# Loading k and v for two heads at a time from another DMA queue, with a reordered last tile, in a low-rank attention decode kernel

## The chip, the cores and the metric

The kernel runs on one core of one Trainium2 chip. The metric is the device time of one execution, in microseconds (us), as the median of several executions. The span of a profile runs from the first to the last instruction of one execution; the measured time exceeds it by about 1.7 to 2.2 us.

PE is TensorE, the matrix engine; DVE, ACT, POOL and SP are VectorE, ScalarE, GpSimd and SyncE. An eviction copies a matmul's result (vp_a, say) into a tile that a later matmul reads (vp_a_sb). A load has landed when all 16 DMA engines have reported their share of it.

## The reference

```python
B, H, Sq, Skv, Dh, R = 1, 16, 1, 8192, 256, 16          # all bf16
kp = einsum("rn,bhnd->bhrd", e_proj, k)                 # 16 x 256 per head
vp = einsum("rn,bhnd->bhrd", f_proj, v)
scores = einsum("bhqd,bhrd->bhqr", q, kp) * Dh ** -0.5
o = einsum("bhqr,bhrd->bhqd", softmax(scores), vp)      # 1 x 256 per head
```

Every byte of k and v is read once: 16 heads, two tensors, 4 MB each, 134.2 MB in all. The arithmetic on it is small. A tuned kernel can therefore only be as fast as its loads, plus what comes before the first byte and after the last one.

## The kernel before

A head's 8,192 rows lie on 128 partitions, 64 consecutive rows on each, so one partition's share is a run of 32 KB. All k and v tiles come from GpSimd's DMA queue into five buffers of 4 MB. The last head's k is loaded first and its v last, in pieces.

```python
KV_BUFS = 5;  RING = "gpsimd"                            # kv_dma = nc.gpsimd
def load_full(dst, src_head):
    kv_dma.dma_start(out=dst[:], in_=src_head.rearrange("(p j) d -> p j d", j=J))   # J = 64

def proj_pairs(acc_a, acc_b, w_t, kt):
    for j in range(JH):                                  # JH = 32: rows j and j + 32 side by side
        j2 = j + JH
        nc.tensor.matmul(acc_a[0:R, :], lhsT=w_t[:, j, :], rhs=kt[:, j, :],
                         start=(j == 0), stop=(j == JH - 1), tile_position=(0, 0))
        nc.tensor.matmul(acc_b[32:32 + R, :], lhsT=w_t[:, j2, :], rhs=kt[:, j2, :],
                         start=(j2 == JH), stop=(j2 == J - 1), tile_position=(0, 32))
# ... k_phase: evict both halves, transpose, add, scores, softmax, transpose p (one head) ...
def v_phase(h, vt, pT_a, pT_b):
    proj_pairs(vp_a, vp_b, f_t, vt)
    # ... evict vp_a and vp_b, two products with p, copy, add into o_sb[:, h, :] ...

# ... the other 15 heads: k_phase, v_phase, loads issued ahead ...
bounds = [0, JH, JH + JH // 2, J - 4, J]                 # the last tile: 0, 32, 48, 60, 64
for a, b in zip(bounds[:-1], bounds[1:]):
    kv_dma.dma_start(out=vt_last[:, a:b, :], in_=v_last[:, a:b, :])
v_phase(h_first, vt_last, pT_first[0], pT_first[1])
nc.sync.dma_start(out=..., in_=o_sb)                     # 8 KB
```

The two matmuls of a step sit in different column tiles of the array and run at the same time (in the trace a pair starts within 0.01 us, as at 66.44 us).

## Time and profile before

| | before |
|---|---|
| median time | 330.81 us (4 runs) |
| span | 329.1 us |
| the k/v queue's packets, share of the time of 16 DMA engines | 96.1% |
| first load packet / last load packet | 2.62 / 321.98 us |
| PE busy, DVE busy | 61%, 19% |

Lines of the profile page of the kernel before: span, busy time by engine, the span in 40 slices (DMA is the busy share of the 16 DMA engines in tenths), queues (packets, MB, share) and the chain that ended last by engine.

```profile
span 329.1 us, 4843 instructions
PE 200.8 (61%) x2210; PEld 139.2 (42%) x2210; DVE 63.1 (19%) x228; ACT 7.0 (2%) x33; POOL 21.9 (7%) x44
...
DMA  7999999999999999999999999999999999999970
GB/s 259 383 442 432 406 438 440 436 402 435 440 446 408 426 440 438 416 426 438 436 422 420 438 436 430 424 430 440 415 431 432 442 408 434 432 442 418 413 312 4
...
q0 software_dynamic: 5168, 134.75, 96.1%
q8 instruction: 17, 0.28, 0.3%
...
DMA 83%; PE 14%; issue 1%; DVE 1%; POOL 0%; POOLq 0%
```

DMA is at nine tenths or more in all slices but the first and the last two. So the middle of this kernel is bound by the rate of the DMA engines, and only the two ends are open to a change. The line of q8: 17 packets of 16 KB in which the engines' own instructions are fetched by the same DMA engines.

The chain that ended last, at the end of the kernel before (start us, duration us, what):

```profile
267.82 43.35 DMA vt<-in_v_dram
...
318.80 2.06 PE vp_a L100 x18
...
321.19 0.99 PE vp_b L108 x10
...
323.72 1.86 PE vp_b L108 x16
...
326.37 0.41 DVE o_sb L226
```

The last load packet lands at 321.98 us, but the chain goes back to a load that landed at 311.2, head 14's v. From there on PE has work until 325.6 us, with gaps of about half a microsecond around the evictions: it works off 6.3 us of head 14 (5.3 us of it at half clock), then the last tile. Those 64 matmuls stand in runs of one column tile (x18, x10, x16), where each takes 0.11 us alone instead of 0.11 us for a pair. Then come the evictions and the output:

```profile
322.99 0.41 DVE L208 CAST vp_a_sb<-vp_a 16x256 bf16<-16x256 f32 x1 [3.73 <-PE vp_a L100]
323.76 0.41 DVE L225 COPY o_a_sb<-o_a_ps 1x256 f32<-1x256 f32 x1 [0.36 <-PE o_a_ps L213]
325.60 0.42 DVE L210 CAST vp_b_sb<-vp_b 16x256 bf16<-16x256 f32 x1 [1.43 <-PE vp_b L108]
326.37 0.41 DVE L226 TENSOR_TENSOR o_sb<-o_a_sb,o_b_ps 1x256 bf16<-1x256 f32 x1 [0.35 <-PE o_b_ps L217]
326.81 0.30 SPq L254 DMA_DIRECT2D out_dram<-o_sb  x1
```

(DVE's and SyncE's timeline; in brackets the idle time before, and what ended it.)

### The profile page before, as it was taken

Reading aid. Unit: us, or ns where it says so; the run is one execution under the profiler, and the core shown is the slowest. Engines: PE = TensorE matmul, PEld = TensorE weight load, DVE = VectorE, ACT = ScalarE, POOL = GpSimd, SP = SyncE. Lnnn points to the kernel's source line nnn. Section 1 sums busy time; section 2 is a strip of 40 time slices with the busy share of each in tenths; the row PEclk is TensorE's granted clock in tenths of the full one; section 3 lists DMA queues with packets and bytes.
Section 4 is the critical chain, followed back from the end, with each engine's and each line's share of the span. In section 5 each row is a group of like instructions: output and inputs, shape, how many; then the busy total and the mean of one; then the engine's idle time right before and its main releaser. Section 6 shows DMA issues by size and latency. Waiting matters only on the chain.

```text
span 329.1 us, 4843 instructions
## 1 busy us (share of the span) xinstructions
PE 200.8 (61%) x2210; PEld 139.2 (42%) x2210; DVE 63.1 (19%) x228; ACT 7.0 (2%) x33; POOL 21.9 (7%) x44
## 2 busy tenths in 40 slices
PE   0067545577666576656677564577666666665695
PEld 0044434455444345534454343345434444443463
DVE  0121222210122221122212022221122222012222
ACT  1000000000000000000000000000000000000000
POOL 7000000000000000000000000000000002000000
PEclk9997789875677977767767678977567787776779
DMA  7999999999999999999999999999999999999970
GB/s 259 383 442 432 406 438 440 436 402 435 440 446 408 426 440 438 416 426 438 436 422 420 438 436 430 424 430 440 415 431 432 442 408 434 432 442 418 413 312 4
DMA packets 5190, 135.06 MB, mean 410 GB/s; under 512 B 609, under 2 KB 625, under 8 KB 945
## 3 DMA queue, kind: packets, MB, share of 16 engines
q0 software_dynamic: 5168, 134.75, 96.1%
q8 instruction: 17, 0.28, 0.3%
q14 instruction: 3, 0.02, 0.0%
q1 hardware_dynamic: 2, 0.01, 0.0%
HBM read 134.75 MB, written 0.01 MB: 410 GB/s over the span
## 4 chain that ended last, share of the span: by engine, by line
DMA 83%; PE 14%; issue 1%; DVE 1%; POOL 0%; POOLq 0%
DMA kt<-in_k_dram 40%; DMA vt<-in_v_dram 39%; PE kp_a L100 6%; PE vp_a L100 6%; DMA e_x<-in_e_proj_dram 4%; PE vp_b L108 1%; PE kp_b L108 0%; DVE e_t L61 0%; DVE vp_a_sb L208 0%; POOL kt_first L50 0%; PE o_a_ps L213 0%; PE o_b_ps L217 0%; DVE vp_b_sb L210 0%; DVE o_sb L226 0%; POOLq L272 0%
## 5 line engine op out<-in xcount | busy, mean ns | idle before, releaser
L100 PE MATMUL kp_a<-kt,e_t 128*16 128x256 bf16 x480 | 84.5, 359 | 47.4 <-DMA kt<-in_k_dram 47.4
L100 PE MATMUL vp_a<-vt,f_t 128*16 128x256 bf16 x480 | 84.1, 358 | 14.3 <-DMA vt<-in_v_dram 14.2
L108 PE MATMUL kp_b<-kt,e_t 128*16 128x256 bf16 x480 | 84.6, 360 | 0.0
L108 PE MATMUL vp_b<-vt,f_t 128*16 128x256 bf16 x480 | 84.2, 359 | 0.0
L100 PEld LDWEIGHTS <-e_t 128*16 128x16 bf16 x512 | 59.0, 116 | 50.7 <-DVE e_t L61 16.5
L108 PEld LDWEIGHTS <-e_t 128*16 128x16 bf16 x512 | 58.6, 117 | 42.6 <-issue 42.5
L100 PEld LDWEIGHTS <-f_t 128*16 128x16 bf16 x512 | 58.2, 114 | 21.0
L108 PEld LDWEIGHTS <-f_t 128*16 128x16 bf16 x512 | 57.7, 115 | 15.3 <-issue 14.7
L123 DVE CAST kp_a_sb<-kp_a 16x256 bf16<-16x256 f32 x16 | 6.6, 412 | 117.4 <-PE kp_b L108 117.4
L208 DVE CAST vp_a_sb<-vp_a 16x256 bf16<-16x256 f32 x16 | 6.6, 412 | 97.2 <-PE vp_b L108 93.4
L95 POOL DMA_DIRECT2D kt<-in_k_dram x15 | 8.0, 531 | 125.3 <-PE vp_b L108 110.7
L95 POOL DMA_DIRECT2D vt<-in_v_dram x15 | 7.9, 529 | 122.1 <-PE kp_b L108 112.2
L179 PE MATMUL pT_a_ps<-ident_b,p_b 1*16 1x1 bf16 x16 | 2.7, 166 | 21.4 <-DVE p_b L176 21.4
L100 PE MATMUL kp_a<-kt_first,e_t 128*16 128x256 bf16 x32 | 5.1, 337 | 16.5 <-DVE e_t L61 16.5
L179 PEld LDWEIGHTS <-p_b 1*16 1x16 bf16 x16 | 1.3, 82 | 23.2 <-DVE p_b L176 23.2
L165 ACT ACTIVATE p_f<-s_ps,nbias 1x16 f32<-1x16 f32 x16 | 4.2, 264 | 302.1 <-DVE nbias L162 302.1
L213 PE MATMUL o_a_ps<-vp_a_sb,pT_a 16*1 16x256 bf16 x16 | 4.2, 265 | 8.0 <-DVE vp_a_sb L208 8.0
L130 PE MATMUL psT_a<-ident_b,kp_a_sb 16*128 16x16 bf16 x32 | 3.2, 171 | 7.0 <-DVE kp_a_sb L123 7.0
L210 DVE CAST vp_b_sb<-vp_b 16x256 bf16<-16x256 f32 x16 | 6.7, 417 | 1.9 <-PE vp_b L108 1.4
L226 DVE TENSOR_TENSOR o_sb<-o_a_sb,o_b_ps 1x256 bf16<-1x256 f32 x16 | 6.5, 409 | 1.9 <-PE o_b_ps L217 0.4
L125 DVE CAST kp_b_sb<-kp_b 16x256 bf16<-16x256 f32 x16 | 6.7, 417 | 0.5
L225 DVE COPY o_a_sb<-o_a_ps 1x256 f32<-1x256 f32 x16 | 6.6, 412 | 0.8 <-PE o_a_ps L213 0.4
(40 smaller groups left out, 70.6 us busy)
## 6 DMA issues: line engine op xcount, KB each, us to landing
kt<-in_k_dram POOLq DMA_DIRECT2D x15, 4096.0 KB, 43.0
vt<-in_v_dram POOLq DMA_DIRECT2D x15, 4096.0 KB, 43.1
kt_first<-in_k_dram POOLq DMA_DIRECT2D x1, 4096.0 KB, 12.9
vt_last<-in_v_dram POOLq DMA_DIRECT2D x1, 2048.0 KB, 38.3
vt_last<-in_v_dram POOLq DMA_DIRECT2D x1, 1024.0 KB, 40.2
vt_last<-in_v_dram POOLq DMA_DIRECT2D x1, 768.0 KB, 42.9
e_x<-in_e_proj_dram POOLq DMA_DIRECT2D x1, 256.0 KB, 13.5
f_x<-in_f_proj_dram POOLq DMA_DIRECT2D x1, 256.0 KB, 13.4
```

Source lines behind the costliest of these rows:

```text
L95: kv_dma.dma_start(out=dst[:], in_=src_head.rearrange("(p j) d -> p j d", j=J))
L100: nc.tensor.matmul(acc_a[0:R, :], lhsT=w_t[:, j, :], rhs=kt[:, j, :], start=(j == 0), stop=(j == JH - 1), tile_position=(0, 0),)
L108: nc.tensor.matmul(acc_b[32 : 32 + R, :], lhsT=w_t[:, j2, :], rhs=kt[:, j2, :], start=(j2 == JH), stop=(j2 == J - 1), tile_position=(0, 32),)
L123: nc.vector.tensor_copy(out=kp_a_sb[:], in_=kp_a[0:R, :])
L125: nc.vector.tensor_copy(out=kp_b_sb[32 : 32 + R, :], in_=kp_b[32 : 32 + R, :])
L165: nc.scalar.activation(out=p_f[:, :], in_=s_ps[:, :], func=mybir.ActivationFunctionType.Exp, bias=nbias[:, :], scale=scale, accum_out=rows ...
L179: nc.tensor.matmul(pT_a_ps[:, :], lhsT=p_b[:, :], rhs=ident_1, is_transpose=True, start=True, stop=True)
L208: nc.vector.tensor_copy(out=vp_a_sb[:], in_=vp_a[0:R, :])
L210: nc.vector.tensor_copy(out=vp_b_sb[32 : 32 + R, :], in_=vp_b[32 : 32 + R, :])
L213: nc.tensor.matmul(o_a_ps[:, :], lhsT=pT_a[0:R, 0:1], rhs=vp_a_sb[0:R, :], start=True, stop=True)
L225: nc.vector.tensor_copy(out=o_a_sb[:, :], in_=o_a_ps[:, :])
L226: nc.vector.tensor_add(out=o_sb[:, h, :], in0=o_a_sb[:, :], in1=o_b_ps[:, :])
```

## The change

Its intent is to handle two heads at a time: 512-column matmuls instead of 256, half the PE instructions, fewer evictions, loads from SyncE's queue, and a last tile that is consumed in the order in which it arrives.

```diff
-    KV_BUFS = 5        # tiles of 4 MB
-    RING = "gpsimd"
+    KV_BUFS = 2        # tiles of 8 MB: [P, 2 heads, J, Dh]
+    RING = "sync"      # e, f and q stay on GpSimd's queue
...
+    # 32 columns, the upper 16 zero: a projection then also writes zeros to partitions 16-31
+    e_t = consts.tile([P, J, 2 * R], bf16)      # f_t too
...
+    def proj_pairs(acc, w_t, kvt, consecutive=False):
+        if consecutive:  ja, jb = range(0, J, 2), range(1, J, 2)
+        else:            ja, jb = range(0, JH), range(JH, J)
+        for j, j2 in zip(ja, jb):
+            nc.tensor.matmul(acc[0:2 * R, :], lhsT=w_t[:, j, :], rhs=kvt[:, :, j, :], ...)
+            nc.tensor.matmul(acc[32:32 + R, :], lhsT=w_t[:, j2, 0:R], rhs=kvt[:, :, j2, :], ...)
...  (one product with an identity that adds the halves; evictions of head 0 on DVE, of head 1 on ACT)
+    # v of the last-but-one pair in pieces [0, 16, 32, 48, 64], consecutive=True
-    bounds = [0, JH, JH + JH // 2, J - 4, J]
+    dma_pair(vt_last, v, first_pair, [0, 24, 40, 52, 60, 64])
+    v_phase(first_pair, vt_last, pT_first, consecutive=True)
```

The diff is cut to its core: dots stand for code left out, and some lines are joined.

More of the change, by code (lines that the diff above doesn't have):

```diff
@@ L27 @@
     assert B == 1 and Sq == 1
-    assert Skv % P == 0 and Dh % P == 0
+    assert Skv % P == 0 and Dh % P == 0 and H % 2 == 0
     DHP = Dh // P
@@ L31 @@
     JH = J // 2
+    NHP = 2
     scale = float(Dh) ** -0.5
@@ L35 @@
     X = mybir.AxisListType.X
-    KV_BUFS = int(os.environ.get("LRP_BUFS", "5"))
-    RING = os.environ.get("LRP_RING", "gpsimd")
+    KV_BUFS = int(os.environ.get("LRP_BUFS", "2"))
+    RING = os.environ.get("LRP_RING", "sync")
     consts = ctx.enter_context(tc.tile_pool(name="consts", bufs=1))
@@ L46, with head_rows @@
     aux_dma = kv_dma if RING == "gpsimd" else nc.gpsimd
-    h_first = H - 1
-    kt_first = kvpool.tile([P, J, Dh], bf16, tag="kv")
-    kv_dma.dma_start(out=kt_first[:], in_=k[0, h_first].rearrange("(p j) d -> p j d", j=J))
+    def head_rows(src, h):
+        return src[0, h].rearrange("(p j) d -> p j d", j=J)
+    pairs = [(2 * i, 2 * i + 1) for i in range(H // 2)]
+    first_pair = pairs[-1]
+    other_pairs = pairs[:-1]
+    kt_first = kvpool.tile([P, NHP, J, Dh], bf16, tag="kv")
+    for hh, h in enumerate(first_pair):
+        kv_dma.dma_start(out=kt_first[:, hh], in_=head_rows(k, h))
     e_x = consts.tile([P, R, J], bf16)
@@ L57 @@
     aux_dma.dma_start(out=q_hd[:], in_=q.rearrange("b h s d -> (b s h) d"))
-    e_t = consts.tile([P, J, R], bf16)
-    f_t = consts.tile([P, J, R], bf16)
-    nc.vector.tensor_copy(out=e_t[:], in_=e_x[:].rearrange("p r j -> p j r"))
-    nc.vector.tensor_copy(out=f_t[:], in_=f_x[:].rearrange("p r j -> p j r"))
+    e_t = consts.tile([P, J, 2 * R], bf16)
+    f_t = consts.tile([P, J, 2 * R], bf16)
+    nc.vector.memset(e_t[:], 0.0)
+    nc.vector.memset(f_t[:], 0.0)
+    nc.vector.tensor_copy(out=e_t[:, :, 0:R], in_=e_x[:].rearrange("p r j -> p j r"))
+    nc.vector.tensor_copy(out=f_t[:, :, 0:R], in_=f_x[:].rearrange("p r j -> p j r"))
     I48 = 48
@@ L77 @@
     nc.vector.tensor_copy(out=ident_b[:], in_=ident_f[:])
-    ident_a = ident_b[0:R, 0:R]
-    ident_hi = ident_b[32 : 32 + R, 32 : 32 + R]
+    sum_id = consts.tile([I48, R], bf16)
+    nc.vector.tensor_add(out=sum_id[:], in0=ident_b[:, 0:R], in1=ident_b[:, 32 : 32 + R])
     ident_1 = ident_b[0:1, 0:1]
@@ L92 @@
     o_sb = consts.tile([1, H, Dh], out.dtype)
-    def load_full(dst, src_head):
-        kv_dma.dma_start(out=dst[:], in_=src_head.rearrange("(p j) d -> p j d", j=J))
-    def proj_pairs(acc_a, acc_b, w_t, kt):
-        for j in range(JH):
-            j2 = j + JH
+    N2 = NHP * Dh
+    def proj_pairs(acc, w_t, kvt, consecutive=False):
+        if consecutive:
+            ja = list(range(0, J, 2))
+            jb = list(range(1, J, 2))
+        else:
+            ja = list(range(0, JH))
+            jb = list(range(JH, J))
+        for j, j2 in zip(ja, jb):
             nc.tensor.matmul(
-                acc_a[0:R, :],
+                acc[0 : 2 * R, :],
                 lhsT=w_t[:, j, :],
-                rhs=kt[:, j, :],
-                start=(j == 0),
-                stop=(j == JH - 1),
+                rhs=kvt[:, :, j, :],
+                start=(j == ja[0]),
+                stop=(j == ja[-1]),
                 tile_position=(0, 0),
@@ L108, in proj_pairs, with copy_on @@
             nc.tensor.matmul(
-                acc_b[32 : 32 + R, :],
-                lhsT=w_t[:, j2, :],
-                rhs=kt[:, j2, :],
-                start=(j2 == JH),
-                stop=(j2 == J - 1),
+                acc[32 : 32 + R, :],
+                lhsT=w_t[:, j2, 0:R],
+                rhs=kvt[:, :, j2, :],
+                start=(j2 == jb[0]),
+                stop=(j2 == jb[-1]),
                 tile_position=(0, 32),
             )
-    def k_phase(h, kt, persist=False):
-        kp_a = psum_acc.tile([R, Dh], f32, tag="kp_a")
-        kp_b = psum_acc.tile([I48, Dh], f32, tag="kp_b")
-        proj_pairs(kp_a, kp_b, e_t, kt)
-        kp_a_sb = work.tile([R, Dh], bf16, tag="kp_a_sb")
-        nc.vector.tensor_copy(out=kp_a_sb[:], in_=kp_a[0:R, :])
-        kp_b_sb = work.tile([I48, Dh], bf16, tag="kp_b_sb")
-        nc.vector.tensor_copy(out=kp_b_sb[32 : 32 + R, :], in_=kp_b[32 : 32 + R, :])
-        psT_a = psum_misc.tile([P, DHP, R], bf16, tag="misc")
-        psT_b = psum_misc.tile([P, DHP, R], bf16, tag="misc")
-        for dh in range(DHP):
+    def copy_on(engine, out, in_):
+        if engine == "act":
+            nc.scalar.activation(out=out, in_=in_, func=mybir.ActivationFunctionType.Copy)
+        else:
+            nc.vector.tensor_copy(out=out, in_=in_)
@@ new lines, with k_phase @@
+    ENG = ("dve", "act")
+    def k_phase(pair, kt, persist=False):
+        kp = psum_acc.tile([I48, N2], f32, tag="kp")
+        proj_pairs(kp, e_t, kt)
+        results = []
+        kp_sbs = []
+        for hh in range(NHP):
+            kp_sb = work.tile([I48, Dh], bf16, tag=f"kp_sb{hh}", name="kp_sb")
+            copy_on(ENG[hh], kp_sb[:], kp[:, hh * Dh : (hh + 1) * Dh])
+            kp_sbs.append(kp_sb)
+        for hh, h in enumerate(pair):
+            psT = psum_misc.tile([P, DHP, R], f32, tag="misc")
+            for dh in range(DHP):
+                nc.tensor.matmul(
+                    psT[:, dh, :],
+                    lhsT=kp_sbs[hh][:, dh * P : (dh + 1) * P],
+                    rhs=sum_id[:],
+                    start=True,
+                    stop=True,
+                )
+            kpT_sb = work.tile([P, DHP, R], bf16, tag="kpT_sb")
+            nc.vector.tensor_copy(out=kpT_sb[:], in_=psT[:])
+            s_ps = psum_misc.tile([1, R], f32, tag="misc")
+            for dh in range(DHP):
+                nc.tensor.matmul(
+                    s_ps[:, :],
+                    lhsT=qT_sb[:, dh, h : h + 1],
+                    rhs=kpT_sb[:, dh, :],
+                    start=(dh == 0),
+                    stop=(dh == DHP - 1),
+                )
+            mx = work.tile([1, 1], f32, tag="mx")
+            nc.vector.reduce_max(out=mx[:, :], in_=s_ps[:, :], axis=X)
+            nbias = work.tile([1, 1], f32, tag="nbias")
+            nc.vector.tensor_scalar_mul(out=nbias[:, :], in0=mx[:, :], scalar1=-scale)
+            p_f = work.tile([1, R], f32, tag="p_f")
+            rowsum = work.tile([1, 1], f32, tag="rowsum")
+            nc.scalar.activation(
+                out=p_f[:, :],
+                in_=s_ps[:, :],
+                func=mybir.ActivationFunctionType.Exp,
+                bias=nbias[:, :],
+                scale=scale,
+                accum_out=rowsum[:, :],
+            )
+            rinv = work.tile([1, 1], f32, tag="rinv")
+            nc.vector.reciprocal(out=rinv[:, :], in_=rowsum[:, :])
+            p_b = work.tile([1, 3, R], bf16, tag="p_b")
+            nc.vector.tensor_scalar_mul(
+                out=p_b[:], in0=p_f[:].unsqueeze(1).to_broadcast([1, 3, R]), scalar1=rinv[:, :]
+            )
+            pT_ps = psum_misc.tile([I48, 1], f32, tag="misc")
@@ L130, in k_phase @@
             nc.tensor.matmul(
-                psT_a[:, dh, :],
-                lhsT=kp_a_sb[0:R, dh * P : (dh + 1) * P],
-                rhs=ident_a,
-                is_transpose=True,
+                pT_ps[:, :],
+                lhsT=p_b[:].rearrange("p a r -> p (a r)"),
+                rhs=ident_1,
                 start=True,
@@ L137, in k_phase @@
             )
-            nc.tensor.matmul(
-                psT_b[:, dh, :],
-                lhsT=kp_b_sb[32 : 32 + R, dh * P : (dh + 1) * P],
-                rhs=ident_hi,
-                is_transpose=True,
-                start=True,
-                stop=True,
-            )
-        kpT_sb = work.tile([P, DHP, R], bf16, tag="kpT_sb")
-        nc.vector.tensor_copy(out=kpT_sb[:], in_=psT_a[:])
-        nc.vector.tensor_add(out=kpT_sb[:], in0=kpT_sb[:], in1=psT_b[:])
-        s_ps = psum_misc.tile([1, R], f32, tag="misc")
@@ L151, in k_phase @@
-        for dh in range(DHP):
-            nc.tensor.matmul(
-                s_ps[:, :],
-                lhsT=qT_sb[:, dh, h : h + 1],
-                rhs=kpT_sb[:, dh, :],
-                start=(dh == 0),
-                stop=(dh == DHP - 1),
-            )
-        mx = work.tile([1, 1], f32, tag="mx")
-        nc.vector.reduce_max(out=mx[:, :], in_=s_ps[:, :], axis=X)
-        nbias = work.tile([1, 1], f32, tag="nbias")
-        nc.vector.tensor_scalar_mul(out=nbias[:, :], in0=mx[:, :], scalar1=-scale)
@@ L163, in k_phase @@
-        p_f = work.tile([1, R], f32, tag="p_f")
-        rowsum = work.tile([1, 1], f32, tag="rowsum")
-        nc.scalar.activation(
-            out=p_f[:, :],
-            in_=s_ps[:, :],
-            func=mybir.ActivationFunctionType.Exp,
-            bias=nbias[:, :],
-            scale=scale,
-            accum_out=rowsum[:, :],
-        )
-        rinv = work.tile([1, 1], f32, tag="rinv")
-        nc.vector.reciprocal(out=rinv[:, :], in_=rowsum[:, :])
-        p_b = work.tile([1, R], bf16, tag="p_b")
@@ L176, in k_phase @@
-        nc.vector.tensor_scalar_mul(out=p_b[:, :], in0=p_f[:, :], scalar1=rinv[:, :])
-        pT_a_ps = psum_misc.tile([R, 1], bf16, tag="misc")
-        nc.tensor.matmul(
-            pT_a_ps[:, :], lhsT=p_b[:, :], rhs=ident_1, is_transpose=True, start=True, stop=True
-        )
-        pT_b_ps = psum_misc.tile([I48, 1], bf16, tag="misc")
-        nc.tensor.matmul(
-            pT_b_ps[32 : 32 + R, :],
-            lhsT=p_b[:, :],
-            rhs=ident_1,
-            is_transpose=True,
-            start=True,
-            stop=True,
-            tile_position=(0, 32),
-        )
@@ L192, in k_phase @@
-        if persist:
-            pT_a = consts.tile([R, 1], bf16)
-            pT_b = consts.tile([I48, 1], bf16)
-        else:
-            pT_a = work.tile([R, 1], bf16, tag="pT_a")
-            pT_b = work.tile([I48, 1], bf16, tag="pT_b")
-        nc.vector.tensor_copy(out=pT_a[:, :], in_=pT_a_ps[:, :])
-        nc.vector.tensor_copy(out=pT_b[32 : 32 + R, :], in_=pT_b_ps[32 : 32 + R, :])
-        return pT_a, pT_b
-    def v_phase(h, vt, pT_a, pT_b):
-        vp_a = psum_acc.tile([R, Dh], f32, tag="vp_a")
-        vp_b = psum_acc.tile([I48, Dh], f32, tag="vp_b")
-        proj_pairs(vp_a, vp_b, f_t, vt)
-        vp_a_sb = work.tile([R, Dh], bf16, tag="vp_a_sb")
-        nc.vector.tensor_copy(out=vp_a_sb[:], in_=vp_a[0:R, :])
-        vp_b_sb = work.tile([I48, Dh], bf16, tag="vp_b_sb")
-        nc.vector.tensor_copy(out=vp_b_sb[32 : 32 + R, :], in_=vp_b[32 : 32 + R, :])
-        o_a_ps = psum_misc.tile([1, Dh], f32, tag="misc")
-        nc.tensor.matmul(
-            o_a_ps[:, :], lhsT=pT_a[0:R, 0:1], rhs=vp_a_sb[0:R, :], start=True, stop=True
-        )
-        o_b_ps = psum_misc.tile([1, Dh], f32, tag="misc")
-        nc.tensor.matmul(
-            o_b_ps[:, :],
-            lhsT=pT_b[32 : 32 + R, 0:1],
-            rhs=vp_b_sb[32 : 32 + R, :],
-            start=True,
-            stop=True,
-        )
-        o_a_sb = work.tile([1, Dh], f32, tag="o_a_sb")
-        nc.vector.tensor_copy(out=o_a_sb[:, :], in_=o_a_ps[:, :])
-        nc.vector.tensor_add(out=o_sb[:, h, :], in0=o_a_sb[:, :], in1=o_b_ps[:, :])
@@ L228 @@
-    pT_first = k_phase(h_first, kt_first, persist=True)
-    heads = list(range(H - 1))
-    def issue_head_dmas(h):
-        kt = kvpool.tile([P, J, Dh], bf16, tag="kv", name="kt")
-        load_full(kt, k[0, h])
-        vt = kvpool.tile([P, J, Dh], bf16, tag="kv", name="vt")
-        load_full(vt, v[0, h])
-        return kt, vt
-    pending = {0: issue_head_dmas(0)}
-    for h in heads:
-        if h + 1 in heads:
-            pending[h + 1] = issue_head_dmas(h + 1)
-        kt, vt = pending.pop(h)
-        pT_a, pT_b = k_phase(h, kt)
-        v_phase(h, vt, pT_a, pT_b)
@@ L247 @@
-    vt_last = kvpool.tile([P, J, Dh], bf16, tag="kv")
-    v_last = v[0, h_first].rearrange("(p j) d -> p j d", j=J)
-    bounds = [0, JH, JH + JH // 2, J - 4, J]
-    for a, b in zip(bounds[:-1], bounds[1:]):
-        kv_dma.dma_start(out=vt_last[:, a:b, :], in_=v_last[:, a:b, :])
-    v_phase(h_first, vt_last, pT_first[0], pT_first[1])
+            if persist:
+                pT = consts.tile([I48, 1], bf16, name=f"pT_keep{h}")
+            else:
+                pT = work.tile([I48, 1], bf16, tag="pT", name="pT")
@@ new lines, in k_phase, with v_phase @@
+            nc.vector.tensor_copy(out=pT[:, :], in_=pT_ps[:, :])
+            results.append(pT)
+        return results
+    def v_phase(pair, vt, pTs, consecutive=False):
+        vp = psum_acc.tile([I48, N2], f32, tag="vp")
+        proj_pairs(vp, f_t, vt, consecutive=consecutive)
+        for hh, h in enumerate(pair):
+            vp_sb = work.tile([I48, Dh], bf16, tag=f"vp_sb{hh}", name="vp_sb")
+            copy_on(ENG[hh], vp_sb[:], vp[:, hh * Dh : (hh + 1) * Dh])
+            o_ps = psum_misc.tile([1, Dh], f32, tag="misc", name="o_ps")
+            nc.tensor.matmul(o_ps[:, :], lhsT=pTs[hh][:, 0:1], rhs=vp_sb[:], start=True, stop=True)
+            copy_on(ENG[hh], o_sb[:, h, :], o_ps[:, :])
@@ new lines, with dma_pair, issue_pair_dmas @@
+    pT_first = k_phase(first_pair, kt_first, persist=True)
+    def dma_pair(dst, src, pair, bounds):
+        for a, b in zip(bounds[:-1], bounds[1:]):
+            for hh, h in enumerate(pair):
+                kv_dma.dma_start(out=dst[:, hh, a:b, :], in_=head_rows(src, h)[:, a:b, :])
+    FULL = [0, J]
+    def issue_pair_dmas(pair, v_bounds=None):
+        kt = kvpool.tile([P, NHP, J, Dh], bf16, tag="kv", name="kt")
+        dma_pair(kt, k, pair, FULL)
+        vt = kvpool.tile([P, NHP, J, Dh], bf16, tag="kv", name="vt")
+        dma_pair(vt, v, pair, v_bounds or FULL)
+        return kt, vt
@@ new lines @@
+    PIECES = [0, 16, 32, 48, 64]
+    n_pairs = len(other_pairs)
+    pending = {}
+    if other_pairs:
+        pending[0] = issue_pair_dmas(other_pairs[0], PIECES if n_pairs == 1 else None)
+    for i, pair in enumerate(other_pairs):
+        if i + 1 < n_pairs:
+            last = i + 1 == n_pairs - 1
+            pending[i + 1] = issue_pair_dmas(other_pairs[i + 1], PIECES if last else None)
+        kt, vt = pending.pop(i)
+        pTs = k_phase(pair, kt)
+        v_phase(pair, vt, pTs, consecutive=(i == n_pairs - 1))
@@ L254 @@
+    vt_last = kvpool.tile([P, NHP, J, Dh], bf16, tag="kv")
+    dma_pair(vt_last, v, first_pair, [0, 24, 40, 52, 60, 64])
+    v_phase(first_pair, vt_last, pT_first, consecutive=True)
     nc.sync.dma_start(
```

## The prediction

> **What bounds the kernel now.** The loads. The chain that ended last is 83% DMA, 14% PE; the queue view has the load queue at 96.1% of all 16 DMA engines. The DMA packet records show 3,968 packets of 32 KB, each 1.216 us: 431 GB/s for sixteen engines. From 2.6 us (first packet) to about 320.2 us (mean last packet) they are busy almost without gaps: 317.4 us for 134.75 MB, where 431 GB/s alone would take 312.6. PE is busy 61%, DVE 19%.
>
> What is not rate is small: 2.6 us before the first packet; about 4 us of slow packets (the first ones, the 128 B runs of e and f, semaphore writes, 17 instruction fetches of 16 KB); the slowest engine ends at 322.0, 1.8 us after the mean; then 7.1 us to the end at 329.1. In that tail (timeline) PE works off a backlog: it takes head 14's v from 311.2, mostly at half clock, starts vt_last only at 318.1 and ends at 325.6. Then DVE to 326.8, and the output DMA, 2.3 us.
>
> **What the change does.**
> - Moves k/v loads from GpSimd's queue to SyncE's. The Trainium skill, "DMA: Bandwidth & Descriptors", section "Issuing engines are not separate DMA queues", says that both run on the same 16 engines; so I expect the same 1.21 to 1.22 us per packet. Section "Latency and other measured facts" gives about 0.6 us to the first byte here against 1 us. In this trace the SyncE output DMA had its first packet 0.73 us after issue, GpSimd's first load 1.35. First packet: 1.6 instead of 2.6 us, -1.0.
> - Halves PE's instructions: fewer fetches, -0.6 us of DMA time, and less straggle, -0.7.
> - 512-column matmuls for two heads, two column tiles in one PSUM bank: time per byte unchanged. A step of two heads is about 0.43 us at half clock, 0.22 at full (twice the measured 0.21 and 0.11): 9 to 10 us per 8 MB tile.
> - Two buffers of 8 MB instead of five of 4. A tile lands every 19.3 us and is read in 9 to 10, so the next load is issued with 9 us still queued. With two heads' chains (3.5 us for one now, estimated 6 for two) PE needs 16 of 19.3 us. No stall.
> - The last tile comes in pieces down to 4 rows, consumed in order, so the backlog vanishes. After the last landing: two steps 0.6, eviction 0.42, ACT copy, product and copy 1.2, gaps 0.2, output 2.3: about 4.7 us instead of 7.1, -2.4.
>
> Sum: 329.1 - 1.0 - 0.6 - 0.7 - 2.4 = 324.4 us span; runs exceed it by 1.7, so about 326. Allowing a little for smoother queueing: **325.3 us**, range 321.5 to 328.5. Faster by over 2%: 0.36; within 2%: 0.61; slower: 0.03.
>
> **Signs.** Right: 32 KB packets near 1.216 us; first packet near 1.6 us; DMA share flat, no dip at tile changes; last matmul under 1 us after the last landing; tail near 4.7 us. Wrong: packets of another size or time; idle DMA slices, SyncE waiting on PE until the queue is dry; PE pairs no longer starting together.
>
> **What would break it.** Another packet rate on SyncE's queue, either way (1% is 3 us); column tiles serialising in one bank, making PE the bound; e, f and q, now on a second queue, arriving late and delaying the first tile.

## The result

The changed kernel takes 326.20 us (median of 10 runs, 325.77 to 326.74); the kernel before, in the same rounds and the four earlier runs, 330.85 us (16 runs). The ratio is 0.9868, 95% interval 0.9855 to 0.9881: 1.3% faster, which counts as "within 2%". Here and below a ratio is not quite the ratio of the medians quoted. The span is 324.2 us; the prediction's sum said 324.4. The number that it named, 325.3 us, was 0.9 us too low: it had taken off a little for smoother queueing.

Lines of the profile page of the changed kernel, as above:

```profile
span 324.2 us, 2563 instructions
PE 158.9 (49%) x1122; PEld 65.6 (20%) x1122; DVE 31.0 (10%) x127; ACT 16.0 (5%) x57; POOL 3.5 (1%) x9
...
DMA  8999999999999999999999999999999999999992
...
q1 hardware_dynamic: 6626, 134.23, 97.2%
q0 software_dynamic: 192, 0.53, 0.5%
q8 instruction: 8, 0.13, 0.2%
```

DMA stays at nine tenths with no dip where tiles change: two buffers of 8 MB are enough. The page's list of DMA issues says why: a k load lands 29.2 us after its issue (the median, which falls on a tile's second half), of which the 8 MB of its tile take 19.4, so about 10 us of other loads were still queued ahead of it. And 8 instruction fetches are counted instead of 17. The chain that ended last in the changed kernel, at its end:

```profile
307.01 12.55 DMA vt_last<-in_v_dram
319.57 0.04 issue
319.61 0.39 PE vp L116
320.00 0.24 PE vp L124
320.24 0.02 issue
320.26 0.43 DVE vp_sb L137
320.69 0.02 issue
320.71 0.39 ACT vp_sb L135
...
321.44 0.37 ACT o_sb L135
```

Now the chain waits for the last piece itself: the last load packet ends at 319.06, PE starts at 319.61 and is done with two steps at 320.24. The output DMA is issued at 321.84, against 326.81 before. From the last landing to the end it is 5.1 us instead of 7.1.

The DMA packet records of the trace allow an account of the 4.9 us. "Lag" is the time at 315 us minus the time that the bytes moved so far would take at 431 GB/s (16 engines, 32 KB in 1.216 us).

| | before, us | after, us | difference | predicted |
|---|---|---|---|---|
| first load packet | 2.62 | 1.78 | -0.84 | -1.0 |
| lag at 315 us, beyond the first packet | 3.63 | 3.30 | -0.33 | -0.6 |
| rest of the last landing (engines that are late) | - | - | -1.74 | -0.7 |
| last load packet | 321.98 | 319.06 | -2.92 | -2.3 |
| from there to the end | 7.09 | 5.14 | -1.95 | -2.4 |
| span | 329.07 | 324.20 | -4.87 | -4.7 |

The sum was met by luck: three terms were too large (by 0.16, 0.27 and 0.45 us) and one too small (by 1.04), and they cancelled. That makes the reasons worth testing.

### The profile page after: what moved, and what is told of

It reads as the page before. It is cut to its first block, busy times and chain, and to the rows that moved or that the text cites. A ratio compares the mean times of both kernels' runs of the same rounds, so it can differ in the third digit from the quotient of the medians.

```text
span 324.2 us, 2563 instructions
## 1 busy us (share of the span) xinstructions
PE 158.9 (49%) x1122; PEld 65.6 (20%) x1122; DVE 31.0 (10%) x127; ACT 16.0 (5%) x57; POOL 3.5 (1%) x9
## 4 chain that ended last, share of the span: by engine, by line
DMA 77%; PE 20%; SPq 1%; issue 0%; ACT 0%; DVE 0%
DMA kt<-in_k_dram 68%; PE kp L124 18%; DMA vt_last<-in_v_dram 9%; PE kp L116 2%; SPq L224 1%; SPq L58 0%; DVE vp_sb L137 0%; PE vp L116 0%; ACT vp_sb L135 0%; ACT o_sb L135 0%; PE o_ps L216 0%; PE vp L124 0%
## 5 line engine op out<-in xcount | busy, mean ns | idle before, releaser
L116 PE MATMUL kp<-kt,e_t 128*32 128x512 bf16 x224 | 64.2, 458 | 60.2 <-DMA kt<-in_k_dram 60.2
L116 PE MATMUL vp<-vt,f_t 128*32 128x512 bf16 x224 | 63.4, 449 | 36.4 <-DMA vt<-in_v_dram 36.4
L124 PE MATMUL kp<-kt,e_t 128*16 128x512 bf16 x224 | 64.2, 458 | 0.0
L124 PE MATMUL vp<-vt,f_t 128*16 128x512 bf16 x224 | 63.2, 449 | 0.0
L116 PEld LDWEIGHTS <-e_t 128*32 128x32 bf16 x256 | 28.1, 113 | 66.1 <-DMA kt<-in_k_dram 63.8
L116 PEld LDWEIGHTS <-f_t 128*32 128x32 bf16 x256 | 27.2, 111 | 50.6 <-DMA vt<-in_v_dram 37.4
L124 PEld LDWEIGHTS <-e_t 128*16 128x16 bf16 x256 | 25.8, 103 | 38.8 <-issue 20.3
L124 PEld LDWEIGHTS <-f_t 128*16 128x16 bf16 x256 | 25.0, 102 | 33.7 <-issue 16.9
L116 PE MATMUL vp<-vt_last,f_t 128*32 128x512 bf16 x32 | 9.9, 463 | 7.6 <-DMA vt_last<-in_v_dram 7.6
L124 PE MATMUL vp<-vt_last,f_t 128*16 128x512 bf16 x32 | 9.9, 463 | 0.0
## 6 DMA issues: line engine op xcount, KB each, us to landing
kt<-in_k_dram SPq DMA_DIRECT2D x14, 4096.0 KB, 29.2
```

What stands on the lines that cost most here:

```text
L116: nc.tensor.matmul(acc[0 : 2 * R, :], lhsT=w_t[:, j, :], rhs=kvt[:, :, j, :], start=(j == ja[0]), stop=(j == ja[-1]), tile_position=(0, 0),)
L124: nc.tensor.matmul(acc[32 : 32 + R, :], lhsT=w_t[:, j2, 0:R], rhs=kvt[:, :, j2, :], start=(j2 == jb[0]), stop=(j2 == jb[-1]), tile_positio ...
```

## The experiments

Twelve kernels ran, all correct. Theory: the gain is the sum of small ends (an earlier first packet, fewer instruction fetches and so less late DMA engines, a tail without backlog). Main rival: SyncE's queue moves data better. In the first four runs the kernel before took 330.05 us (11 runs), in the next four 330.53, in the last four 330.01.

### 1. The queue alone

```diff
 (kernel before)
-    RING = "gpsimd"
+    RING = "sync"
```

> The kernel before, with k and v loaded from SyncE's queue and nothing else changed (e, f, q stay on GpSimd's). Theory (the gain is a sum of small ends; the queue gives only an earlier first packet): first packet near 1.8 us instead of 2.6, 32 KB packets still 1.216 us, every later event 0.8 us earlier, the tail unchanged because PE works off its backlog there in unpaired matmuls: about 330.0 us, 0.25% faster. Rival (SyncE's queue moves data better, and the whole gain of the change is the queue): near 326 us. A second question: the slowest DMA engine ended 1.5 us after the others in the kernel before. If that belongs to the GpSimd queue it is gone here; if it belongs to the last instruction fetch, it is still here.

Measured: 330.53 us, ratio 1.0013 (0.9998 to 1.0028): no gain. The rival falls: 32 KB packets took 1,220.4 ns on the mean, as before (1,220.5). But my own number fell too. The first packet did come at 1.77 us, and the lag at 315 us was 5.48 us instead of 6.25; yet head 14's v, on which the end of this kernel hangs, was there for PE at 311.13 us instead of 311.21. The head start was lost to the slowest engine. Each DMA engine ends its share of a load with a small semaphore packet, so the spread between the first and the last engine can be read for each 4 MB load. At the load before the last tile it was 3.84 us in the kernel before and 4.42 here. A load has landed when its last engine has, so bytes moved ahead of time on the other fifteen help nobody. The second question is answered as well: at the last load the slowest engine came 2.1 us after the median one, against 2.2 in the kernel before, so the lateness is not GpSimd's queue.

### 2. The last tile alone

```diff
 (kernel before)
-    bounds = [0, JH, JH + JH // 2, J - 4, J]
+    bounds = [0, 24, 40, 52, 60, 64]
     ... proj_pairs of the last tile: pairs (j, j + 32) -> pairs (2i, 2i + 1)
```

> The kernel before, with only the last tile changed: pieces that end at rows 24, 40, 52, 60, 64 as in the changed kernel, and matmul pairs on rows (0,1), (2,3) ... instead of (0,32), (1,33) .... Queue, buffers and head-by-head work as before. Theory (the tail was bound by PE: 64 matmuls of the last tile alone at 0.11 us each from 318.2 to 325.6 instead of 32 pairs): PE now ends about 1 us after the last landing at 322, then 2 evictions, 2 products, 2 adds and the output, so the span ends near 326.3 instead of 329.1 and the run near 328.0 us, 0.85% faster. Rival (the queue is the gain): same as before within 0.2%.

Measured: 328.87 us, ratio 0.9959 (0.9944 to 0.9974). It is faster, by half of what was expected. The end of its chain:

```profile
282.42 40.45 DMA vt_last<-in_v_dram
322.87 0.04 issue
322.91 0.27 PE vp_a L101
...
324.74 0.41 DVE o_sb L227
```

The backlog is gone as expected: PE takes its last step when the last piece has landed. But the last load packet ends at 322.43 us, no longer hidden behind PE, with the slowest engine 2.6 us after the median one. Removing the backlog exposed the late engine.

### 3. Both

> Both of the above: SyncE's queue and the new last tile, but single heads, five buffers of 4 MB and 4,400 PE instructions. Theory (the gain is start plus tail): the two gains add up, about 327 us, and if the slowest DMA engine's lateness comes from instruction fetches it is still there and leaves the kernel 1 us behind the changed one at 326.2. Rival (the two-head tiles with half the PE instructions are needed): clearly slower than that, 328 us or more.

Measured: 328.18 us, ratio 0.9939 (0.9924 to 0.9954). The last load packet is at 321.39 us, 2.3 us after that of the changed kernel, and the run is 2.0 us slower than the changed one. So the two-head tiles do bring something that neither queue nor tail brings, and it shows in the last landing. At the last load the slowest engine came 2.9 us after the mean of the sixteen, in the changed kernel 1.2; these 1.7 us make up the 2.3 together with 0.6 us (an estimate) for 32 KB packets that took 1,220.4 ns on the mean instead of 1,218.1, over 257 per engine.

### 4. The queue undone

```diff
 (changed kernel)
-    RING = "sync"
+    RING = "gpsimd"
```

> The changed kernel with k and v, and so e, f and q too, on GpSimd's queue. Theory: first packet 0.8 to 1.0 us later, all else equal, so about 327.1 us, 0.3% slower than the changed kernel, still about 1.1% faster than before. Rival (the queue is the gain): back to 330 us.

Measured: 326.63 us, ratio 0.9889 (0.9872 to 0.9905), against 0.9868 for the changed kernel; the intervals overlap. The first packet is at 2.65 us and the last at 319.56. The queue is worth about 0.2% of the 1.3%, and even with it undone the landing is far earlier than in the three kernels built on the one before.

### 5. One and two instruction fetches more

The count of fetches is 17 before 319 us in all kernels of single heads, and 8 in the changed one (9 in two of the runs that follow). The 16 engines' arrival times at the end of a 4 MB load, in the kernel before, ns after the first engine, just before and just after the ninth fetch (at 177.7 us):

```
load done at 173.1 us:  0 354 495 514 567 647 814 1495 1909 1955 2011 2046 2054 2130 2209 2289
load done at 184.1 us:  0 354 495 521 574 647 821 1502 1909 1955 2011 2046 2131 2209 2290 3603
```

One engine alone moves, from 2,054 to 3,603 ns; the others keep their places for 10 us to within a few ns. 2.05 us was also the spread that the first fetch had left behind. The spread rises by more than 1 us at the first, ninth and seventeenth fetch, and by at most 0.2 us at any other. After sixteen fetches, at 310.7 us, eight engines stand at 3.45 to 3.84 us and the other eight at 0 to 2.47. That suggests that fetches take turns on eight engines, and that the delay stays, as it would if every engine has its own share of each load and none takes over another's.

The packet records show what the delay consists of. The ninth fetch takes 1,086 ns, and the load packet that starts 14 ns before its end takes 1,694 ns instead of 1,216: 1,086 - 14 + 1,694 - 1,216 = 1,550 ns, the step seen above. They support the turns too: the two durations differ from one fetch to the next, and come back to within 2 ns eight fetches later (1,086 and 1,694 at the first and the ninth, 1,018 and 1,756 at the third and the eleventh).

```diff
 (changed kernel, while PE waits for q)
+    for _ in range(128):      # 256 in the second run
+        nc.tensor.matmul(pad_ps[:, :], lhsT=pad_sb[:], rhs=pad_sb[:], start=True, stop=True)
```

> The changed kernel with 128 tiny matmuls (256 PE instructions, 16 columns each) on a zeroed tile put first, while PE is idle until q lands at 23 us. They change no data and end before 23 us. They add one 16 KB instruction fetch, so the last fetch before the end, at 290 us, is the ninth instead of the eighth. Theory (fetches take turns on 8 of the 16 DMA engines, and each holds its engine back about 1.2 us that is never made up, as the jumps of the spread at the first, ninth and seventeenth fetch suggest): spread between first and last engine at the 4 MB loads about 2 us until 290 and about 3.2 us after it, last landing about 320.3 instead of 319.1, run near 327.3 us instead of 326.2. Rival (a fetch costs only its bytes, 16 KB of 134.75 MB): plus 0.04 us, not to be seen.

> The same with 256 tiny matmuls, two more fetches. Theory: the ninth and tenth fetch hit two different engines once more, so the slowest engine is no later than in the run with one more fetch: again near 327.3 us, not 328.4. A cost that is linear in fetches would give the latter. The tiny matmuls should still end near 20 us; if they last beyond 23 us they delay the first tile, but not the end.

Measured: one more fetch 326.87 us, ratio 0.9895 (0.9882 to 0.9907), last load packet at 319.91 us; two more 327.26 us, ratio 0.9902 (0.9889 to 0.9915), last load packet at 320.10. Against the changed kernel (0.9868, 319.06) that is +0.27% and +0.84 us for the first, and only +0.07% and +0.19 us more for the second. The rival, bytes only (0.04 us), is out, and so is a cost that is linear in fetches. The unused tile also moves the k/v tiles by 32 bytes (see section 7), but the 32 KB packets kept their mean, 1,218.2 ns against 1,218.1.

The cost in the landing is smaller than I wrote (0.84, not 1.2), and the arrival times show why. Here they have to be sorted by the semaphore that each load reports to, and not by time alone: the small loads of the tail follow each other so closely that one load's first engines arrive before the last engine of the one ahead. Sorted so, the ninth fetch sets one engine back by 1.5 us in both runs, as in the kernel before. In the first run, at 290 us, it goes from about 1,650 to 3,185 ns, and the spread is still 3.1 us at the last load (2.3 in the changed kernel, 5.1 in the kernel before). But the slowest engine had been another one, at 2,378 ns, so the landing loses only the 0.8 us between 2,378 and 3,185. In the second run the ninth fetch, at 264 us, takes the spread to 3.4 us, and the tenth, at 292 us, only brings a second engine level with the first (3,389 and 3,398 ns), at almost no cost. That the turns go over just eight engines stays an inference, because the records do not name the engine.

### 6. The row order of the tail undone in the changed kernel

```diff
 (changed kernel)
-    dma_pair(vt_last, v, first_pair, [0, 24, 40, 52, 60, 64]);  consecutive=True
+    dma_pair(vt_last, v, first_pair, [0, 32, 48, 60, 64]);      consecutive=False
     ... and the v tile ahead of it whole, consecutive=False
```

> The changed kernel with the order of the tail undone: the last tile in the pieces of the kernel before (ends at rows 32, 48, 60, 64), pairs of rows (0,32), (1,33) ..., and the v tile ahead of it whole. Here PE keeps the pairs together. Theory (in the kernel before, the tail was long because its matmuls ran unpaired and began late, not because of the order of rows): only the 4 pairs of the last piece are left after the last landing instead of 2, and fewer small packets come before: 326.2 plus 0.4 minus 0.4, so 326 to 327 us. Rival (the row order is what shortens the tail): 328 us or more.

Measured: 328.84 us, ratio 0.9961 (0.994 to 0.9981). The rival was right. The last load packet even comes earlier (318.52 us), but PE is late. Windows of this run: PE and PEld busy, DVE, ACT and POOL busy, granted clock, DMA share, GB/s:

```profile
312.00:316.00 4.00, 2.06 (x10) 0.79 (x12) 0.00 (x0) 0.00 (x0) 0.00 (x0) 0.50 1.00 411
316.00:320.00 4.00, 4.00 (x30) 1.76 (x28) 0.00 (x0) 0.00 (x0) 0.00 (x0) 0.75 0.35 134
320.00:324.00 4.00, 3.35 (x29) 1.39 (x25) 0.61 (x2) 0.38 (x1) 0.00 (x0) 1.00 0.02 4
```

And DVE's timeline of this run, at the first eviction of the last head (start, duration, operation; in brackets the idle time before it and what ended it):

```profile
323.04 0.42 DVE L137 CAST vp_sb<-vp 48x256 bf16<-48x256 f32 x1 [13.03 <-PE vp L124]
```

Each pair (j, j + 32) needs a row of the second half, so PE can do no more than one matmul with the first 32 rows until 313.94 us, when rows 32 to 47 are there:

```profile
313.94 0.59 PE L124 MATMUL vp<-vt_last,f_t 128*16 128x512 bf16 x1 [3.65 <-DMA vt_last<-in_v_dram]
```

All 32 steps then fall into the last 9 us, and they start at half clock (0.50): nine steps of 0.43 us. The same windows of the changed kernel:

```profile
308.00:312.00 4.00, 4.00 (x22) 1.26 (x18) 0.00 (x0) 0.00 (x0) 0.00 (x0) 0.54 1.00 413
312.00:316.00 4.00, 2.14 (x20) 0.83 (x20) 0.00 (x0) 0.00 (x0) 0.00 (x0) 1.00 1.01 409
316.00:320.00 4.00, 2.68 (x24) 0.83 (x20) 0.00 (x0) 0.00 (x0) 0.00 (x0) 1.00 0.48 186
```

Here the cold steps are done with the first piece, at 308 to 312 us, and only warm steps are left. The Trainium skill, "TensorE: Matmul & The Clock Gate", Part 1, says that an idle window of about 3.4 us throttles PE to half clock and that about as long a busy time releases it; this trace agrees, with 3.65 us of waiting before 313.94, a clock of 0.50 after it and shorter steps from 317.7 on, 3.8 us later. So my reading of the tail before as a matter of unpaired matmuls was at most part of it: pairs in the old row order are as long a tail. What shortens it is that rows are consumed in the order in which they land. This run undid the sizes of the pieces along with the order, so what each is worth alone is not shown; that the order is the main part is read from the wait above.

### 7. Going further

The run named best keeps the changed kernel and edits its end.

```diff
 (changed kernel)
-    PIECES = [0, 16, 32, 48, 64]
+    PIECES = [0, 32, 64]
+    # early, once p of the last pair is known: g[n] = sum_r p[r] * f[r, n] for the last 4 rows j
     v_phase of the last tile:
-        all 64 rows -> vp -> evict -> product with p -> copy
+        60 rows -> vp -> evict -> product with p into o_ps (start)
+        for j in 60..63: matmul(o_ps, lhsT=g[:, j], rhs=vt_last[:, hh, j, :])   # accumulates
+        copy o_ps -> output
+    heads 0 to 13 are written out before; the last output is 1 KB
```

> A version that goes on from the changed kernel where the runs say time is left. The v tile before the last in 2 pieces instead of 4 (16 KB packets instead of 8 KB, about -0.3 us of DMA time). For the last 4 rows of the last tile the weights f and the softmax p are multiplied ahead, so that their share of the output is a product straight into the output accumulator: after the last landing come 8 small matmuls, one copy and the output, instead of 2 pairs, 2 evictions, a product, a copy and the output (about -1.0 us). The first 14 heads are written out earlier, so that the last output packet is 1 KB instead of 8 KB (-0.27 us). Expected 324.6 to 325.2 us, about 0.4% below the changed kernel; correct within the reference's tolerance.

Measured: 324.10 us (the median of its four fast runs), ratio 0.9808 (0.9795 to 0.9821), faster than either kernel and than I expected; the interval holds 0.98, so whether it is 2% is left unclear. But the lag at 315 us was 3.65 us, 1.4 less than in the changed kernel, which nothing in this edit explains: almost all 32 KB packets took exactly 1,213 ns. What differed was the address of the k/v tiles in SBUF: the edit's small constants had moved them to a multiple of 256 bytes. The next four runs test that by an unused tile in front of them, with nothing else changed.

```diff
+    shift = consts.tile([P, n], bf16)        # 192, 224, 64 and 256 bytes per partition
+    nc.vector.memset(shift[:], 0.0)
```

> The changed kernel with an unused tile of 192 bytes per partition in front of the k/v tiles, and nothing else. It moves the k/v tiles in SBUF from 64 to 0 bytes past a multiple of 256 (their address is in the compiled program). Theory: rows that begin on a multiple of 256 bytes are written with less waste, which is why the 32 KB packets took 1.213 us throughout in the run named best, 1.218 on the mean in the changed kernel and 1.220 in the one before. Expected: mean packet 1.2138 instead of 1.218, 254 such packets per engine, so about 1.1 us less: 325.1 us. Rival (the packets of best were faster for another reason, such as the chip or the smaller tail): 326.2 us, packets 1.218.

> The kernel before with an unused tile of 224 bytes per partition in front of the k/v tiles, which moves them from 32 to 0 bytes past a multiple of 256. Theory: packets 1.2138 instead of 1.2204 us on the mean, about 1.6 us less up to the landing of head 14's v, on which its end hangs: about 329.0 us, 0.5% faster. Rival: unchanged, 330.5 us.

> The run named best, with 64 unused bytes per partition in front of the k/v tiles, which puts them 64 bytes past a multiple of 256 again, as in the changed kernel. Theory: packets back at 1.218 us, run near 325.2 us instead of 324.2; what is left against 326.2 is what the new end of the kernel is worth, about 1.0 us. Rival: 324.2 us as before.

> The run named best with 256 unused bytes more, so that the k/v tiles begin on a multiple of 512 instead of an odd multiple of 256. If 256 is the unit, there is no change: 324.2 us, packets 1.2138.

| kernel | k/v address, bytes past a multiple of 256 | mean 32 KB packet, 30 to 280 us | time, us | ratio (95%) |
|---|---|---|---|---|
| before | 32 | 1,220.5 ns | 330.01 | 1 |
| before, shifted (b_align) | 0 | 1,215.6 | 329.01 | 0.9959 (0.9943 to 0.9975) |
| changed | 64 | 1,218.1 | 326.20 | 0.9868 (0.9855 to 0.9881), other rounds |
| changed, shifted (a_align) | 0 | 1,214.2 | 324.75 | 0.9830 (0.9813 to 0.9847) |
| best, shifted away (best_mis) | 64 | 1,218.1 | 325.71 | 0.9862 (0.9844 to 0.9880) |
| best | 0 | 1,214.2 | 324.10 | 0.9808 (0.9795 to 0.9821), other rounds |
| best, multiple of 512 (best_512) | 0 | 1,214.3 | 324.28 | 0.9822 (0.9804 to 0.9841) |

The theory holds in all four. An unused tile of 192 bytes makes the changed kernel about 0.4% faster, and 64 bytes take the same from best. 512 is no better than 256. The pages of the changed kernel and of the shifted one show the same bytes in a shorter span:

```profile
DMA packets 6828, 134.91 MB, mean 416 GB/s; under 512 B 785, under 2 KB 801, under 8 KB 1697
DMA packets 6829, 134.91 MB, mean 418 GB/s; under 512 B 786, under 2 KB 802, under 8 KB 1698
```

(The second line is the shifted one's.) The Trainium skill, "DMA: Bandwidth & Descriptors", section "How a descriptor splits into AXI transactions", says that the first transaction of a descriptor which does not start 256-byte aligned starts at the 256-byte boundary below, at the cost of extra beats. That fits the unit of 256 found here. But the page speaks of bytes that are read, and here it was the written side that moved; that this is the cause of these 4 to 5 ns per packet is not shown.

What the new end itself is worth is best_mis against the changed kernel (0.9862 against 0.9868, 0.5 us by the medians), or best_512 against a_align, in the same rounds (0.9822 against 0.9830, also 0.5 us): far from the 1.0 to 1.6 expected, and the intervals overlap. The timeline of best shows why:

```profile
316.60 0.39 PE L116 MATMUL vp<-vt_last,f_t 128*32 128x512 bf16 x1 [0.97 <-DMA vt_last<-in_v_dram]
...
317.68 0.42 DVE L137 CAST vp_sb<-vp 48x256 bf16<-48x256 f32 x1 [14.09 <-PE vp L124]
318.13 0.38 ACT L135 ACTIVATE vp_sb<-vp 48x256 bf16<-48x256 f32 x1 [14.17 <-DVE vp_sb L137]
...
319.71 0.37 ACT L135 ACTIVATE o_fin<-o_fin_ps 1x256 bf16<-1x256 f32 x1 [1.20 <-PE o_fin_ps L286]
320.11 0.32 SPq L298 DMA_DIRECT2D out_dram<-o_fin  x1
```

The piece of rows 52 to 59 is there for PE at 316.60 us, and its steps and evictions (to 318.51) now outlast the last landing at 317.57: the chain moved one piece back. And the 1 KB output took as long from issue to the end (322.4 - 320.11 = 2.3 us) as the 8 KB one did (329.1 - 326.81 = 2.3 us).

## Why the prediction was right

- **The bound, and no gain from the queue's rate.** Right. 32 KB packets had a median of 1,215 ns after and 1,216 before; the queue alone gave 1.0013, the queue undone 0.9889 against 0.9868. This agrees with the Trainium skill, "DMA: Bandwidth & Descriptors", section "Issuing engines are not separate DMA queues", which says that loads run on the same 16 DMA engines whichever engine starts them.
- **First packet.** -0.84 us measured, -1.0 predicted. The SyncE load had its first packet 1.02 us after issue (0.76 to 1.78), not 0.73 as the output DMA had suggested. That the term reaches the end was shown only where the slowest engine lets it: it did nothing for the kernel before (run 1).
- **Fewer instruction fetches.** The mechanism was right and the sizes were off. The prediction took -0.6 us for DMA time and -0.7 for the straggle. The packet records sum to 317.4 us per engine before and 317.5 after; at 315 us the lag beyond the first packet was 0.33 us less. The rest of the landing, engines that are late, was -1.74 us. By the semaphores, the slowest engine reported the last load 2.8 us after the mean of the sixteen before and 1.2 us after it now. The prediction gave the straggle less than half of that; in the runs one fetch more, on an engine that already had one, put the last landing off by 0.84 us. No run takes fetches out of the kernel before, so that they are the whole of the 1.74 us is argued from these spreads and not shown.
- **An effect that was not in the sum.** The change also moved the k/v tiles from 32 to 64 bytes past a multiple of 256, by the accident of other tiles' sizes, and the mean packet fell from 1,220.5 to 1,218.1 ns. That is 0.6 us over the 257 packets' worth of 32 KB per engine (an estimate from these two means). But only part of it is the address. Without the packets over 1,300 ns (17 before and 8 after from 30 to 280 us, at the instruction packets of q8 and q14) the means are 1,217.9 and 1,216.8 ns, and both kernels have 1,213.0 on a multiple of 256. So the address gave 1.0 ns, or 0.3 us (an estimate), and fewer fetches the rest. Together they made up for the 8 KB packets of the new pieces, which at 312 ns are slower per byte than the large ones (four take 1,248 ns).
- **Two buffers.** Right: about 10 us of queue ahead of each k load, 9 predicted, and no idle DMA slice.
- **Tail.** -1.95 us measured, -2.4 predicted. From the start of PE's last steps (319.61) to the end it is 4.6 us, the predicted 4.7. The term left out the 0.54 us between the end of the last packet and PE's start. As to its reason, the order of rows is what counts: taken back together with the pieces, the kernel takes 328.84 us, and most of the gain is gone.

The prediction treated its terms as a sum. They were a chain of alternatives: in the kernel before, PE's backlog hid the late engine; removing the backlog alone gave 0.41% and the queue alone nothing, while the changed kernel, with fewer fetches as well, gained 1.32%.

## What to carry to other kernels

When a kernel is bound by loads, look at the last engine and not at the mean: a load has landed when the slowest of the 16 DMA engines has, and here the delay from an instruction fetch (1.5 us on one engine) was not made up later, so fewer instructions can shorten even a DMA-bound kernel. Consume the last tile in the order in which its pieces land, and see that PE has its half-clock steps behind it before the last piece comes. Check the SBUF address of large load targets: starting them on a multiple of 256 bytes was worth 0.4% here for one unused tile, as much as the reordered tail alone gave the kernel before.

## What the Trainium skill lacked or had wrong

- "DMA: Bandwidth & Descriptors" gives the 256-byte rule in beats of the bytes that are read, but no time, and nothing on where an SBUF tile that is written starts. Here 32 KB packets took 1,217.9 ns on the mean at 32 bytes past a multiple of 256, 1,216.8 at 64 and 1,213.0 at 0, leaving out those over 1,300 ns.
- "Runtime: NRT & Kernel Launch", Terms, says that instruction memory is refilled in 16 KiB blocks, and the runs agree (16,384 bytes each). Its section "Instruction fetch mechanics" calls the cost of crossing a block boundary mostly hidden, and no page says what a refill costs the loads on its DMA engine. Here one engine was delayed lastingly, from 2,054 to 3,603 ns after the first engine at one fetch, and one fetch more put the last landing off by 0.84 us.
- "DMA: Bandwidth & Descriptors", Queues, rings and completion order, puts refills in queue row 14. In these traces they are 17 (before) and 8 (after) packets of 16 KB on q8; q14 has 3 and 2 instruction packets of 8 KB. Whether the profile's queue numbers are the page's rows is not shown.
- "DMA: Bandwidth & Descriptors", Latency and other measured facts, gives about 0.6 us to the first byte from SyncE and 1 us from GpSimd. The first load packet came 1.02 us and 1.35 us after its issue, at the start of the kernel; the output DMA's came 0.73 us after.
- The same section says that DMA engines 7 and 15 are usually slower, and gives contention from GpSimd's descriptor rings as a best guess. Here the spread between engines was as large on SyncE's queue (4.42 us in run 1, against 3.84 us on GpSimd's), and grew at instruction fetches. The records do not name the engine, so this does not test which engines are slow.
